# The last six chunks' product with w_out by one level of Strassen's algorithm

## The chip, the cores and the metric

The kernel runs on one core of a Trainium2 chip. The metric is the time on the device in microseconds (us). The engines work side by side, each through its own list in order: PE (TensorE, matrix products), DVE (VectorE), ACT (ScalarE), POOL (GpSimd) and SP (SyncE, which here only starts transfers).

## The reference

An attention over 4 batches, 8 heads, 768 positions and 64 values per head. Three of the heads see all earlier positions, the others only the first 4 and a window of 64. Its output, laid out as 3072 tokens by 512, goes through two dense products with a gate between them:

```python
def _moe_ref(x, w_in, w_out, beta):
    h = x @ w_in                                   # 3072x512 @ 512x2048
    g = h * (1.0 / (1.0 + np.exp(-beta * h)))
    return (g @ w_out).astype(np.float32)          # 3072x2048 @ 2048x512
```

The change concerns only the last line.

## The kernel before

The 3072 tokens are 8 chunks (NCHUNK) of 384, each a half of a batch's positions, so three tiles of 128 tokens. Each chunk has four units of attention (a unit is a pair of heads). For a unit `steps_QK` makes scores on PE and their exponentials on ACT, DVE multiplies masks into them (L509 to L527), `steps_PV` multiplies with the values, and `normalize` divides on DVE (`rec`, `x`, L572 and L576).

The first dense product, `steps_G1`, has 16 steps per chunk, one for each 128 of the 2048 columns (FO = 16 blocks): four matmuls of 384 columns into a bank of PSUM (L631), a tanh on ACT (`th`, L636), and the "gate" on DVE (L639), which writes the block `fi` of `gT[c]`, a bf16 tile of 128 x 16 x 384. A bank is free again after its gate. The second product, `steps_G2`, has four steps per token tile, each of four matmuls of 512 columns over four blocks (L684); after the fourth, ACT copies the bank to `osb` (L688) and SP stores it (L690). The very last tile is cut in 256, 128 and 128 columns (L669, L675, L677). Factor 0.5 in these copies belongs to the gate's formula.

PSUM has three pools: `ps_m` with three banks ("mm"), `ps_s` with two double banks ("sp"), `ps_o` with one.

The order of the work on every engine is written out by hand. `RAMP` is the list of words for the start, and `PLAN` has one line for each unit from unit 8 on: `V` a visit of scores, `p` a product with the values, `a` or `A` a step of the first product (with a bank of `ps_m` or `ps_s`), `b` a step of the second. `feed` takes the next step of the list `first` or `second`; where a `b` finds no step ready it runs an `a`, and the other way round. Gates, masks and loads are put off by `later` by a delay in the plan's own clock, which counts the steps' nominal costs, and a step that needs them runs them first. POOL makes the copies of values (`VX`, `VO`, L253 to L262) and issues the row loads of the next chunk's keys and queries (L284); SP issues the transposes, loads of v and stores.

## Time and profile before

| what | us |
|---|---|
| median of three runs | 228.47 (228.04 to 228.51) |
| profiled execution: span from the first to the last instruction | 226.6 |
| PE busy in it | 220.1 |
| ACT, DVE, POOL busy | 154.4, 138.7, 87.7 |
| matmuls of the second product with 512 columns (368) | 85.9 busy |
| granted PE clock over the span | 1.000 |

The profiled execution's own time is not given beside its span; the median is 1.9 us above it. A matmul's busy time is from its start to the end of its results, and the next one starts before that, so that 368 matmuls of 379 ns each took less than 368 x 379 ns of the time line. "Idle before" in a row of a group is the time that the engine waited ahead of these instructions, and behind the arrow stands whom it waited for. The chain is followed back from the last instruction through whatever ended last at each step.

### The profile page before, as it was taken

The page shows a single profiled execution, that of the slowest core. Times are in us where ns is not written, and L with a number is a line of the kernel's source. Part 1 is how long each engine was busy: PE and PEld are TensorE (multiplying, and loading weights), DVE is VectorE, ACT ScalarE, POOL GpSimd, SP SyncE. Part 2 cuts the span into 40 slices and gives each one's busy share as a digit, 9 for nine tenths or more (in the row PEclk, how much of TensorE's full clock was granted, in tenths as well). Part 3 has the DMA queues.
Part 4 walks back from the last instruction along what each step waited for, and adds up shares of the span by engine and source line. Part 5 has one row for each costly group of instructions (what it writes and reads, how often), then busy time and mean ns, then how long its engine had stood idle before and what let it go on. Part 6 is the DMA issues. An engine that isn't in the chain of part 4 may idle for free.

```text
span 226.6 us, 5028 instructions
## 1 busy us (share of the span) xinstructions
PE 220.1 (97%) x1918; PEld 126.5 (56%) x1918; DVE 138.7 (61%) x341; ACT 154.4 (68%) x253; POOL 87.7 (39%) x139
## 2 busy tenths in 40 slices
PE   8889999999999999999999999999999999999993
PEld 3556666644655665556644665556645565456553
DVE  2578898862674779357932699457854768038600
ACT  4689788846768897449933887669875887148521
POOL 4578940459272399143069019930520000000000
PEclk9999999999999999999999999999999999999999
DMA  6999999999999799999779986999704030110012
GB/s 205 253 307 226 201 209 232 197 223 178 145 211 179 159 158 140 126 188 155 86 132 153 152 192 77 127 157 144 178 4 127 4 81 0 49 74 19 0 56 87
DMA packets 95384, 31.67 MB, mean 140 GB/s; under 512 B 81776, under 2 KB 92416, under 8 KB 95360
## 3 DMA queue, kind: packets, MB, share of 16 engines
q1 hardware_dynamic: 58880, 22.82, 50.1%
q0 software_dynamic: 35904, 8.13, 41.3%
q10 hardware_dynamic: 576, 0.40, 0.5%
q8 instruction: 15, 0.25, 0.5%
q14 instruction: 9, 0.07, 0.1%
HBM read 27.27 MB, written 6.29 MB: 148 GB/s over the span
## 4 chain that ended last, share of the span: by engine, by line
PE 87%; DMA 6%; SPq 3%; POOL 1%; issue 0%; ACTq 0%; ACT 0%; POOLq 0%
PE mm L684 36%; PE mm L631 24%; PE sp L631 12%; PE po L563 6%; PE sp L482 6%; DMA vs<-in_v_dram 5%; DMA s<-in_q_dram 2%; PE mm L669 2%; SPq L133 1%; SPq L120 1%; PE mm L482 1%; PE mm L353 1%; PE mm L601 1%; POOL VX L253 1%; POOL VO L262 0%
## 5 line engine op out<-in xcount | busy, mean ns | idle before, releaser
L684 PE MATMUL mm<-w_out_sb,gT 128*128 128x512 bf16 x368 | 85.9, 379 | 0.0
L491 ACT ACTIVATE es<-sp 128x768 bf16<-128x768 f32 (+2 forms) x72 | 56.5, 834 | 18.3 <-PE sp L482 18.0
L631 PE MATMUL mm<-xT,w_in_sb 128*128 128x384 bf16 x348 | 64.5, 326 | 0.0
L631 PEld LDWEIGHTS <-w_in_sb 128*128 128x128 bf16 x512 | 47.8, 98 | 29.7 <-issue 0.2
L636 ACT ACTIVATE th<-mm,beta_h 128x384 f32<-128x384 f32 x87 | 49.6, 587 | 6.4 <-DVE Mh L238 1.0
L684 PEld LDWEIGHTS <-gT 128*128 128x128 bf16 x368 | 33.4, 98 | 36.0 <-issue 1.5
L639 DVE SCALAR_TENSOR_TENSOR gT<-th,mm 128x384 bf16<-128x384 f32 x87 | 46.8, 552 | 7.6 <-ACT th L636 3.8
L631 PE MATMUL sp<-xT,w_in_sb 128*128 128x384 bf16 x164 | 32.3, 326 | 0.0
L688 ACT ACTIVATE osb<-mm 128x512 f32<-128x512 f32 x23 | 13.8, 602 | 25.5 <-PE mm L684 25.2
L563 PEld LDWEIGHTS <-es 128*128 128x128 bf16 x472 | 23.5, 98 | 12.5 <-issue 0.9
L253 POOL CAST VX<-vs 128x512 bf16<-128x512 f32 x15 | 9.4, 627 | 51.6 <-DMA vs<-in_v_dram 42.0
L639 DVE SCALAR_TENSOR_TENSOR gT<-th,sp 128x384 bf16<-128x384 f32 x41 | 22.3, 552 | 5.7 <-ACT th L636 3.7
L636 ACT ACTIVATE th<-sp,beta_h 128x384 f32<-128x384 f32 x41 | 23.8, 586 | 2.3 <-PE sp L631 0.2
L563 PE MATMUL po<-VX,es 128*128 128x65 bf16 x360 | 25.1, 194 | 0.0
L284 POOL DMA_DIRECT2D s<-in_q_dram x30 | 22.5, 779 | 4.0 <-DMA w_out_sb<-in_moe_w_out_dram 4.0
L284 POOL DMA_DIRECT2D s<-in_k_dram x30 | 22.3, 757 | 3.6 <-DMA w_in_sb<-in_moe_w_in_dram 3.4
L572 DVE RECIPROCAL rec<-po 128x6 f32<-128x6 f32 x28 | 5.4, 192 | 28.0 <-PE po L563 27.9
L482 PE MATMUL sp<-QTD,KT 64*128 64x128 bf16 (+2 forms) x258 | 18.9, 240 | 0.0
L509 DVE TENSOR_TENSOR es<-es,Mh 128x768 bf16<-128x768 bf16 (+1 forms) x26 | 15.6, 628 | 5.0 <-ACT es L491 4.4
L576 DVE TENSOR_TENSOR x<-po,rec 128x384 bf16<-128x384 f32 x28 | 15.6, 557 | 1.0
L482 PEld LDWEIGHTS <-KT 64*128 64x128 bf16 x278 | 11.1, 94 | 5.7 <-issue 3.7
L261 POOL COPY VO<-VX 128x512 bf16<-128x512 bf16 x16 | 9.7, 629 | 6.0 <-DVE VX L253 6.0
(74 smaller groups left out, 156.1 us busy)
## 6 DMA issues: line engine op xcount, KB each, us to landing
vs<-in_v_dram SPq DMA_DIRECT2D x24, 256.0 KB, 5.3
out_dram<-osb SPq DMA_DIRECT2D x23, 256.0 KB, 2.8
w_in_sb<-in_moe_w_in_dram POOLq DMA_DIRECT2D x4, 512.0 KB, 9.6
w_out_sb<-in_moe_w_out_dram POOLq DMA_DIRECT2D x4, 512.0 KB, 17.0
s<-in_k_dram POOLq DMA_DIRECT2D x30, 64.0 KB, 4.3
s<-in_q_dram POOLq DMA_DIRECT2D x30, 64.0 KB, 5.7
s<-in_k_dram SPq DMA_DIRECT2D x4, 384.0 KB, 10.4
s<-in_q_dram SPq DMA_DIRECT2D x4, 384.0 KB, 10.5
```

The source lines that it names most:

```text
L253: copy(out=VX[b % 2][:, h2 * HT + t, :, 0:D], in_=staged["v", c][:, t])
L284: nc.gpsimd.dma_start(out=ROWS[c % 2, name][:, t, i * 4 * D:(i + 1) * 4 * D].rearrange("p (h d) -> p h d", d=D), in_=src[b, i:H:2, r:r + 1 ...
L482: nc.tensor.matmul(sps[i][r][:, x * 128:y * 128], key(a, lhs), s["QT"][half(a), qi * 128:(qi + y - x) * 128], start=first, stop=first or y ...
L491: nc.scalar.activation(out=views[i].rearrange("p r k j -> p r (k j)"), in_=banks[2][:, :, 0:n * 128], func=ACTF.Exp, scale=scale)
L509: eng.tensor_mul(ev[:, :, 0:n], ev[:, :, 0:n], Mh[h2][:, None, m0:m0 + n].to_broadcast([128, 2, n, 128]))
L563: nc.tensor.matmul(po[:, qi, hh, :], e, val, start=(j == 0), stop=(j == len(lst) - 1))
L576: nc.vector.tensor_mul(xg[g][:, :, :, u % 2, :].rearrange("p a t d -> p t a d"), po[:, :, :, 0:D], rec.to_broadcast([128, HT, 2, D]))
L631: nc.tensor.matmul(hp[:, 0:HALF], w_in_sb[:, mo, fi * 128:(fi + 1) * 128], xT[c][:, mo, :], start=(mo == 0), stop=(mo == MO - 1))
L636: nc.scalar.activation(out=th, in_=hp[:, 0:HALF], func=ACTF.Tanh, scale=beta_h[:, fi:fi + 1])
L639: nc.vector.scalar_tensor_tensor(out=gTs[c][:, fi, :], in0=th, scalar=1.0, in1=hp[:, 0:HALF], op0=ALU.add, op1=ALU.mult)
L684: nc.tensor.matmul(op, gTs[c][:, fi, ns * 128:(ns + 1) * 128], w_out_sb[:, fi, :], start=(fi == 0), stop=(fi == FO - 1))
L688: nc.scalar.activation(out=osb, in_=op, func=ACTF.Copy, scale=0.5)
```

## The change

The tokens of chunks 2 to 7 (18 tiles) are multiplied with w_out in nine pairs of tiles. With the pair's two tiles as the upper and lower half of a matrix A, cut in its 2048 columns at the middle (A11, A12 above, A21, A22 below), and w_out cut to B11, B12, B21, B22 of 1024 x 256 each, seven products of 256 columns take the place of eight:

- p1 = A11 B11, then p2 adds A12 B21 into the same bank X: ACT copies X after p1 (half of it is needed alone) and again after p2.
- p6 = S2 T2, then p7 adds N3 T3 into the same bank Y: DVE reads Y after p6 and after p7.
- p5 = S1 T1 into bank Z; p4 = A22 T4 into bank W; p3 adds N4 B22 into Z.

S1 = A21 - A22, S2 = A11 - S1, N3 = A21 - A11 and N4 = A12 - S2 are tensor_tensor operations of 128 x 1024 bf16 on DVE, made per pair by `minus`. The results are put together in `osb` by `plus`, five DVE operations of 128 x 256 per pair (in0 from PSUM, in1 from osb). T1 = B12 - B11, T2 = T1 + B22 (in two halves) and T4 = B21 - T2 are made once, by the new words ws0, ws1 and ws2 in unit 11's line of `PLAN`; T3 = B12 + B22 overwrites B12 at the first pair's start.

Tiles 0 and 1 of a chunk are a pair, and tile 2 of an even chunk goes with tile 2 of the next one. To keep it until then, POOL copies it to `kept` (128 x 2048 bf16) after the even chunk's pair has been issued. The last two pairs are taken step by step in turn. Per pair there are 7 steps of 8 matmuls, 63 steps for these tiles in place of 72 of 4. The loads, the first product and the attention are untouched; `osb` gets a fourth buffer, and two masks share buffers with the new sums.

The diff, with some lines around the edits left out:

```diff
     moe = ctx.enter_context(tc.tile_pool(name="moe", bufs=2))
+    sums = ctx.enter_context(tc.tile_pool(name="sums", bufs=3))
...
 
-    Ns = consts.tile([128, 5 * 128], BF16, name="Ns")
-    Nc = consts.tile([128, 256], BF16, name="Nc")
+    Ns = sums.tile([128, 8 * 128], BF16, name="S")[:, 0:5 * 128]
+    Nc = sums.tile([128, 8 * 128], BF16, name="S")[:, 0:256]
...
                                          start=(fi == 0), stop=(fi == FO - 1))
-                        osb = moe.tile([128, d_model], F32, name="osb", bufs=3)[:, 0:z - a]
+                        osb = moe.tile([128, d_model], F32, name="osb", bufs=4)[:, 0:z - a]
...
-                    osb = moe.tile([128, d_model], F32, name="osb", bufs=3)
+                    osb = moe.tile([128, d_model], F32, name="osb", bufs=4)
...
         return res
 
+    KB = FO // 2
+    wB11, wB12 = w_out_sb[:, 0:KB, 0:256], w_out_sb[:, 0:KB, 256:512]
+    wB21, wB22 = w_out_sb[:, KB:FO, 0:256], w_out_sb[:, KB:FO, 256:512]
+    wT = {}
+    def weight_sums(i):
+        sub = nc.vector.tensor_sub
+        if i == 0:
+            a = stage.tile([128, 2, 4, HT, D], F32, name="s0").rearrange("p n h t d -> p (n h t d)").bitcast(BF16)
+            b = stage.tile([128, 2, 4, HT, D], F32, name="s1").rearrange("p n h t d -> p (n h t d)").bitcast(BF16)
+            wT[1] = [a[:, 0:KB * 256].rearrange("p (f d) -> p f d", f=KB)]
+            wT[4] = [b[:, 0:KB * 256].rearrange("p (f d) -> p f d", f=KB)]
+            wT[2] = [x[:, KB * 256:KB * 384].rearrange("p (f d) -> p f d", f=KB // 2) for x in (a, b)]
+            sub(out=wT[1][0], in0=wB12, in1=wB11)
+        elif i in (1, 2):
+            f = slice((i - 1) * KB // 2, i * KB // 2)
+            nc.vector.tensor_add(out=wT[2][i - 1], in0=wT[1][0][:, f], in1=wB22[:, f])
+            sub(out=wT[4][0][:, f], in0=wB21[:, f], in1=wT[2][i - 1])
+        elif i == 3:
+            nc.vector.tensor_add(out=wB12, in0=wB12, in1=wB22)
+    def weight(n, kb):
+        return {"B11": lambda: w_out_sb[:, kb, 0:256], "T3": lambda: w_out_sb[:, kb, 256:512],
+                "B21": lambda: w_out_sb[:, KB + kb, 0:256], "B22": lambda: w_out_sb[:, KB + kb, 256:512],
+                "T1": lambda: wT[1][0][:, kb], "T4": lambda: wT[4][0][:, kb],
+                "T2": lambda: wT[2][kb // (KB // 2)][:, kb % (KB // 2)]}[n]()
+    kept = {}
+    def keep(c):
+        for f in gates[c]:
+            f()
+        kept[c] = moe.tile([128, FO, 128], BF16, name="kept", bufs=1)
+        nc.gpsimd.tensor_copy(out=kept[c], in_=gTs[c][:, :, 256:384])
+    def steps_seven(lo, hi, before=None, end=False, last=False):
+        h = {}
+        def place_of(x):
+            c, ns = x
+            return (2 * chunks[c][0] + chunks[c][1]) * HALF + ns * 128
+        def sides():
+            for c in (lo[0], hi[0]):
+                for f in gates[c]:
+                    f()
+            if lo[0] in kept:
+                A1 = kept.pop(lo[0])
+            else:
+                A1 = gTs[lo[0]][:, :, lo[1] * 128:(lo[1] + 1) * 128]
+            A2 = gTs[hi[0]][:, :, hi[1] * 128:(hi[1] + 1) * 128]
+            h.update(A11=A1[:, 0:KB], A12=A1[:, KB:FO], A21=A2[:, 0:KB], A22=A2[:, KB:FO])
+        def minus(n, a, b):
+            home = att.tile([128, 8 * 128], BF16, name="es", bufs=11) if end else sums.tile([128, 8 * 128], BF16, name="S")
+            h[n] = home.rearrange("p (f t) -> p f t", f=KB)
+            nc.vector.tensor_sub(out=h[n], in0=h[a], in1=h[b])
+        def mm(p, a, w, first=True, cols=(0, 256)):
+            if first and p not in h:
+                h[p] = ps_m.tile([128, 512], F32, name="mm")[:, 0:cols[1] - cols[0]]
+            for kb in range(KB):
+                nc.tensor.matmul(h[p], h[a][:, kb], weight(w, kb)[:, cols[0]:cols[1]], start=first and kb == 0, stop=kb == KB - 1, skip_group_check=not first)
+        def plus(out, p, other):
+            nc.vector.scalar_tensor_tensor(out=out, in0=h[p], scalar=0.5, in1=other, op0=ALU.mult, op1=ALU.add)
+        def store(x, osb, a=0, z=d_model):
+            n0 = place_of(x)
+            nc.sync.dma_start(out=out[n0:n0 + 128, a:z], in_=osb[:, a:z])
+        def p1():
+            if before is not None:
+                before()
+            sides()
+            h["o1"] = moe.tile([128, d_model], F32, name="osb", bufs=4)
+            h["o2"] = moe.tile([128, d_model], F32, name="osb", bufs=4)
+            mm("X", "A11", "B11")
+            nc.scalar.activation(out=h["o2"][:, 256:512], in_=h["X"], func=ACTF.Copy, scale=0.5)
+            minus("S1", "A21", "A22")
+            minus("S2", "A11", "S1")
+        def p2():
+            mm("X", "A12", "B21", first=False)
+            nc.scalar.activation(out=h["o1"][:, 0:256], in_=h["X"], func=ACTF.Copy, scale=0.5)
+            minus("N3", "A21", "A11")
+        def p6():
+            mm("Y", "S2", "T2")
+            plus(h["o1"][:, 256:512], "Y", h["o2"][:, 256:512])
+        def p7():
+            mm("Y", "N3", "T3", first=False)
+            plus(h["o2"][:, 0:256], "Y", h["o2"][:, 256:512])
+            minus("N4", "A12", "S2")
+        def p5():
+            mm("Z", "S1", "T1")
+            plus(h["o2"][:, 256:512], "Z", h["o2"][:, 0:256])
+        def p4():
+            mm("W", "A22", "T4")
+            plus(h["o2"][:, 0:256], "W", h["o2"][:, 0:256])
+            store(hi, h["o2"])
+        def p3():
+            mm("Z", "N4", "B22", first=False)
+            plus(h["o1"][:, 256:512], "Z", h["o1"][:, 256:512])
+            store(lo, h["o1"])
+        def p5_last():
+            zz = ps_s.tile([128, 2, 512], F32, name="sp")
+            for i in range(2):
+                h[f"Z{i}"] = zz[:, i, 0:128]
+                mm(f"Z{i}", "S1", "T1", cols=(i * 128, i * 128 + 128))
+                plus(h["o2"][:, 256 + i * 128:384 + i * 128], f"Z{i}", h["o2"][:, i * 128:i * 128 + 128])
+            store(hi, h["o2"], 256, 512)
+        def p4_last():
+            mm("W", "A22", "T4")
+            plus(h["o2"][:, 0:256], "W", h["o2"][:, 0:256])
+            store(hi, h["o2"], 0, 256)
+            store(lo, h["o1"], 0, 256)
+        def p3_last():
+            for i in range(2):
+                mm(f"Z{i}", "N4", "B22", first=False, cols=(i * 128, i * 128 + 128))
+                o = h["o1"][:, 256 + i * 128:384 + i * 128]
+                plus(o, f"Z{i}", o)
+                store(lo, h["o1"], 256 + i * 128, 384 + i * 128)
+        return [(8 * 109, f) for f in ((p1, p2, p6, p7, p5_last, p4_last, p3_last) if last else (p1, p2, p6, p7, p5, p4, p3))]
     first, second = [], []
     for c in range(NCHUNK):
         first += [(c, x) for x in steps_G1(c)]
-        second += [(c, x) for x in steps_G2(c)]
+        if c < 2:
+            second += [(c, x) for x in steps_G2(c)]
+        elif c % 2 == 0:
+            second += [(c, x) for x in steps_seven((c, 0), (c, 1), before=(lambda: weight_sums(3)) if c == 2 else None)]
+            second[-1] = (c, (second[-1][1][0], lambda f=second[-1][1][1], c=c: (f(), keep(c))))
+        elif c < NCHUNK - 1:
+            second += [(c, x) for x in steps_seven((c, 0), (c, 1))]
+            second += [(c, x) for x in steps_seven((c - 1, 2), (c, 2))]
+        else:
+            two = steps_seven((c - 1, 2), (c, 2), end=True), steps_seven((c, 0), (c, 1), end=True, last=True)
+            second += [(c, x) for both in zip(*two) for x in both]
 
...
             late[n].pop(0)(copies[eng or "v"])
+        elif what == "ws":
+            weight_sums(n)
...
-        A b A a V ro4 p V a p p ro4 p p p
+        A ws0 b A a V ro4 p V a ws1 p p ro4 ws2 p p p
         b A ro4 a a p V p ro4 p p ro4 b ro4 a a A ro4 A b b b dk4 A V a p dq4 p b A b
```

In the order of the built programs, line numbers of the new one stand a line or more behind the old ones (L631 is L632 there, L684 is L685, L639 is L640). At the second pair (chunk 3, tiles 0 and 1), PE ran this before: the last step of the first product, then steps of the second, with a product of the attention (po) in between.

```order
L631 LDWEIGHTS w_in_sb
L631 MATMUL sp<-xT,w_in_sb 128x384
L684 LDWEIGHTS gT
L684 MATMUL mm<-w_out_sb,gT 128x512 [waits DVE_49]
...
L563 LDWEIGHTS es
L563 MATMUL po<-VX_127,es 128x65
```

Now PE at the same place; the first L766 rows are p1, the one that waits for ACT (Activation_49) is p2's first, the rows with S are p6 (weights from S2, columns from T2 in s_1203), and the last two p7's first.

```order
L564 MATMUL po<-VX_130,es 128x65 [waits PE_49]
L766 LDWEIGHTS gT
L766 MATMUL mm<-w_out_sb,gT 128x256
...
L766 MATMUL mm<-w_out_sb,gT 128x256 [waits Activation_49]
...
L766 LDWEIGHTS S [waits DVE_49]
L766 MATMUL mm<-s_1203,S 128x256
...
L766 LDWEIGHTS S [waits DVE_49]
L766 MATMUL mm<-w_out_sb,S 128x256 [waits DVE_49]
```

Where one step of 512 columns followed another without a wait, p2 now waits for ACT, p6 for DVE's sum, and p7 for DVE's read, with nothing between these products.

DVE at the first pair (chunk 2, tiles 0 and 1) before: the end of a unit (rec and x), the last gate, the next unit's end, and masks.

```order
L572 RECIPROCAL rec<-po 128x6 [waits PE_49]
L576 TENSOR_TENSOR x<-po,rec 128x3x2x64 [waits DVE_49]
L639 SCALAR_TENSOR_TENSOR gT<-th,mm 128x384 [waits Activation_49]
L572 RECIPROCAL rec<-po 128x6 [waits PE_49]
L576 TENSOR_TENSOR x<-po,rec 128x3x2x64 [waits DMAHW7_49,DVE_49]
L509 TENSOR_TENSOR es<-es,Mh_112 128x768 [waits Activation_49] x2
```

And now: L721 is T3, L760 the block sums (S1, S2, N3, and N4 further down), L769 the reads of banks.

```order
L577 TENSOR_TENSOR x<-po,rec 128x3x2x64 [waits DVE_49]
L721 TENSOR_TENSOR w_out_sb<-w_out_sb 128x8x256
L640 SCALAR_TENSOR_TENSOR gT<-th,mm 128x384 [waits Activation_49]
L760 TENSOR_TENSOR S<-gT 128x1024 [waits DVE_49]
L760 TENSOR_TENSOR S<-gT,S 128x1024 [waits DVE_49]
L760 TENSOR_TENSOR S<-gT 128x1024
L769 SCALAR_TENSOR_TENSOR osb<-mm,osb 128x256 [waits DMAHW6_49,PE_49,Activation_49]
L573 RECIPROCAL rec<-po 128x6 [waits PE_49]
L577 TENSOR_TENSOR x<-po,rec 128x3x2x64 [waits DMAHW7_49,DVE_49]
L769 SCALAR_TENSOR_TENSOR osb<-mm,osb 128x256 [waits DMAHW5_49,PE_49]
L760 TENSOR_TENSOR S<-gT,S 128x1024
L510 TENSOR_TENSOR es<-es,Mh_115 128x768 [waits Activation_49] x2
```

T3 stands ahead of the last gate, and two reads of banks and four sums stand ahead of the masks (L510).

POOL at the same place before: the copies of values, then row loads.

```order
L261 COPY VO_129<-VX_127 128x8x64 [waits Pool_49]
L262 COPY VO_129<-VX_127 4x8x64 [waits Pool_49]
L284 DMA s_558<-in_k_dram 128x4x64 [waits DMAHW7_49,DMASW2_49]
L284 DMA s_558<-in_k_dram 128x4x64 [waits DMAHW0_49,DMASW3_49]
L284 DMA s_558<-in_k_dram 128x4x64 [waits DMASW4_49]
L284 DMA s_558<-in_k_dram 128x4x64 [waits DMASW5_49]
```

And now, with `kept`, which waits for the chunk's last gate:

```order
L262 COPY VO_132<-VX_130 128x8x64 [waits Pool_49]
L263 COPY VO_132<-VX_130 4x8x64 [waits Pool_49]
L285 DMA s_561<-in_k_dram 128x4x64 [waits DMAHW7_49,DMASW2_49]
L285 DMA s_561<-in_k_dram 128x4x64 [waits DMAHW0_49,DMASW3_49]
L736 COPY kept<-gT 128x2048 [waits DVE_49]
L285 DMA s_561<-in_k_dram 128x4x64 [waits DMASW4_49]
```

The row loads behind it start when the copy has ended.

## The prediction

> **What bounds the kernel now.** I read the busy times first, then the chain that ended last, then one window over the stretch that the change touches.
>
> ```profile
> PE 220.1 (97%) x1918; PEld 126.5 (56%) x1918; DVE 138.7 (61%) x341; ACT 154.4 (68%) x253; POOL 87.7 (39%) x139
> ...
> PE 87%; DMA 6%; SPq 3%; POOL 1%; issue 0%; ACTq 0%; ACT 0%; POOLq 0%
> ...
> L684 PE MATMUL mm<-w_out_sb,gT 128*128 128x512 bf16 x368 | 85.9, 379 | 0.0
> ```
> ```profile
> 88.50:222.90 134.40, 134.34 (x1110) 76.03 (x1107) 77.53 (x188) 85.97 (x142) 35.87 (x50) 1.00 0.71 101
> ```
>
> TensorE (PE) carries 87% of the chain. From 88.5 us, where chunk 2 starts its product with w_out, to 222.9 us it is busy 134.34 of 134.40 us at the full granted clock (1.00). So every microsecond of matmul taken away there is gained, and every microsecond that PE has to wait is lost: nothing absorbs it. VectorE (DVE) has 77.5 us of work in these 134 us.
>
> **The matmuls saved.** The chain in order of time and the instructions of the last tile price the columns:
>
> ```profile
> 212.41 6.91 PE mm L684 x32
> 219.31 3.55 PE mm L669 x48
> ```
> ```profile
> L669 PE MATMUL mm<-w_out_sb,gT x48: 219/219/273, 219.1 to 222.6; 128*128 128x128 bf16 x32, 128*128 128x256 bf16 x16
> ```
>
> 32 matmuls of 512 columns take 6.91 us, 0.216 each. The last tile's 16 of 256 and 32 of 128 columns take 3.55; with 0.109 and 0.056 they make 1.75 + 1.79 = 3.54, so price goes by columns and a narrow matmul pays no extra for its weights. A pair of token tiles costs 32 x 0.216 = 6.91 now, and 7 products x 8 x 0.109 = 6.12 then: 0.79 saved, nine times 7.1, and 0.1 more because the last tile's split costs less: **-7.2 us**. A rule speaks against this term: the Trainium skill, "TensorE: Matmul & The Clock Gate", section "Back-to-back issue gap", gives about 81 ns for a pair of weight load and matmul at 128 columns and 131 ns at 512. An estimate halfway by columns is 98 ns at 256, and by these a pair would get dearer, 5.5 us in place of 4.2. The rows above (0.216 and 0.056) disagree with it at both ends, so the sum does not use it; as a rival it stands below.
>
> **What the seven products wait for.** I call the pairs 1 to 9 in the order of the program: 1 = chunk 2 tiles 0,1; 2 = chunk 3 tiles 0,1; 3 = tile 2 of both; 4 to 6 the same for chunks 4 and 5; 7 = chunk 6 tiles 0,1; 8 and 9 interleaved at the end. PE takes its instructions in order, so a product that waits holds up all behind it.
>
> *First term: p2 adds into p1's bank.* ScalarE (ACT) must first copy the half-finished bank. In pairs 1 to 6 p2 stands directly behind p1.
>
> ```profile
> 219.15 3.70 PE L669 MATMUL mm<-w_out_sb,gT 128*128 128x256 bf16 x48
> 221.10 0.39 ACT L677 ACTIVATE osb<-mm 128x256 f32<-128x256 f32 x1 [1.15 <-PE mm L669]
> ```
> ```profile
> 7.54 0.48 ACT L364 COPY QTD<-mm 128x384 bf16<-128x384 bf16 x1 [0.39 <-PE mm L353]
> 8.14 0.28 PEld L482 LDWEIGHTS <-KT 64*128 64x128 bf16 x10 [0.42 <-ACT QTD L364]
> ```
>
> The sixteenth 256-column matmul could be followed by another at 219.15 + 1.75 = 220.90; it ends 0.16 later (273 ns long against 109 ns of spacing), and the copy starts at 221.10 and takes 0.39. From the end of an ACT copy (7.54 + 0.48) to the PE instruction that waited are 0.12. Gap: 0.16 + 0.04 + 0.39 + 0.12 = 0.71. In pair 4 two exponentials stand ahead of the copy on ACT:
>
> ```profile
> L491 ACT ACTIVATE es<-sp 128x768 bf16<-128x768 f32 x48 | 37.2, 810 | 14.4 <-PE sp L482 14.1
> ```
>
> With the first still running when p1 begins and a shorter one behind it I take 1.2 there. Pair 7 has two short matmuls in between: 0.65. Pairs 8 and 9 cover each other. 5 x 0.7 + 1.2 + 0.65 = **+5.35**.
>
> *Second term: p7 adds into p6's bank*, which DVE must have read (a scalar_tensor_tensor of 256 columns).
>
> ```profile
> L639 DVE SCALAR_TENSOR_TENSOR gT<-th,mm 128x384 bf16<-128x384 f32 x87 | 46.8, 552 | 7.6 <-ACT th L636 3.8
> L675 DVE TENSOR_SCALAR osb<-mm 128x128 f32<-128x128 f32 x1 | 0.3, 291 | 8.4 <-PE mm L669 8.4
> ```
> ```profile
> 12.97 0.39 DVE L248 CAST qkb<-s 128x384 bf16<-128x384 f32 x1 [1.02 <-DMA s<-in_k_dram]
> 13.41 0.17 PEld L353 LDWEIGHTS <-qkb 128*128 128x128 bf16 x3 [0.88 <-DVE qkb L248]
> ```
>
> 384 columns take 0.552 and 128 take 0.291, so 256 take 0.42. DVE to PE is 13.41 - 13.36 = 0.05, PE to DVE about the same. Gap: 0.16 + 0.06 + 0.42 + 0.05 = 0.7. p7 is directly behind p6 in pairs 2, 3, 5, 6, 7 (3.5); pair 4 has four tiny matmuls between (0.6); pair 1 has attention work of over 1 us there (0); in 8 and 9 the block sums of the other pair keep DVE back (0.5): **+4.6**. The third such place, p3 behind p5, has p4 (0.87 us) between: DVE needs 0.2 + 0.42 + 0.69 + 0.42 = 1.73 after p7, and p3 comes at 1.75; nothing, with no reserve.
>
> *Third term: the block sums come late for p6.* S1 needs the chunk's last gate, S2 needs S1. The three gate rows at the present start of such a stage:
>
> ```profile
> 212.24 5.34 PE L684 MATMUL mm<-w_out_sb,gT 128*128 128x512 bf16 x24
> 212.44 0.58 ACT L636 ACTIVATE th<-sp,beta_h 128x384 f32<-128x384 f32 x1
> 213.06 0.55 DVE L639 SCALAR_TENSOR_TENSOR gT<-th,sp 128x384 bf16<-128x384 f32 x1
> ```
> ```profile
> L509 DVE TENSOR_TENSOR es<-es,Mh x26: 420/554/1676, 21.2 to 186.7; 128x768 bf16<-128x768 bf16 x21, 128x512 bf16<-128x512 bf16 x5
> ```
>
> The last gate ends 1.37 us after the product begins. That is hidden now, since the product wants the gates one by one. A bf16 sum of 768 columns is 0.55 us undisturbed and of 512 is 0.42, so 1024 is 0.69. S1 and S2 end 1.37 + 2 x 0.72 = 2.85 after p1 began; p1, gap and p2 end at 0.87 + 0.71 + 0.87 = 2.45. Pair 2 waits 0.45. In pairs 5 and 7 an x of the attention delays the gates: 0.9 and 0.45. Pairs 3 and 6 need no new gate: 0. Pair 1 has DVE's sum T3 over w_out (2048 columns, 1.22 us by the same slope) and these two ahead of the last gate:
>
> ```profile
> 89.01 0.19 DVE L572 RECIPROCAL rec<-po 128x6 f32<-128x6 f32 x1
> 89.24 0.56 DVE L576 TENSOR_TENSOR x<-po,rec 128x384 bf16<-128x384 f32 x1
> ```
>
> rec and x end 0.9 after p1 begins, T3 at 2.1, the gate at 2.65, S2 at 4.05: 1.6. Together **+3.4**. Behind p5 of pair 1 stand products that need a mask which on DVE comes after two of the new operations (0.42 + 0.69): **+0.95**.
>
> *Fourth term: the copy "kept" on GpSimd (POOL)*, 2048 columns, in pairs 1, 4 and 7. It waits for the same last gate as S1.
>
> ```profile
> 139.16 2.41 DVE L509 TENSOR_TENSOR es<-es,Mh 128x768 bf16<-128x768 bf16 x2
> 139.62 1.68 POOL L262 COPY VO<-VX 4x1536 bf16<-4x1536 bf16 x1
> ```
> ```profile
> 108.09 0.91 DVE L509 TENSOR_TENSOR es<-es,Mh 128x768 bf16<-128x768 bf16 x2
> ```
> ```profile
> L262 POOL COPY VO<-VX 4x1536 bf16<-4x1536 bf16 x4 | 6.1, 1516 | 0.2
> L261 POOL COPY VO<-VX 128x512 bf16<-128x512 bf16 x16 | 9.7, 629 | 6.0 <-DVE VX L253 6.0
> ```
>
> Two mask products take 0.91 us alone and 2.41 beside a POOL copy of 1.68: the second of them ended only after the copy did, 1.50 lost. By 629 ns for 512 columns and 1516 for 1536 the new copy is 1.96. The Trainium skill, "SBUF — State Buffer", section "Who interferes with whom", calls the port pair an exclusive lock between a DVE operation with two SBUF inputs and a GpSimd operation that reads SBUF; by it S2 would lose the whole 1.96 in pairs 1 and 7, 3.9 in place of the 3.0 I take by the row's delay. Worked from the rows alone, the bounds are 0 and 2 x 1.96 = 3.9, and I take the measured delay of 1.50 for pair 1 and pair 7 each (pair 4 none: DMA issues keep POOL from starting the copy beside the sums). **+3.0**.
>
> *The rest.* T1, T2, T4 (five operations on DVE, 1.22 + 4 x 0.69 = 4.0 us) go into the stretch of
>
> ```profile
> 60.00:70.00 10.00, 10.00 (x126) 6.04 (x125) 7.68 (x21) 6.97 (x12) 5.74 (x7) 1.00 1.22 177
> ```
>
> where it has 2.3 us free: 0 to 1.7 over, I take **+0.5**. Two ACT reads of 256 replace two of 512 per pair, off the path: 0. POOL's row loads start up to 2 us later behind "kept"; before they are used lie a whole chunk's steps: 0, at most 1. The plan of steps keeps its words while the products have 63 steps for these tiles in place of 72, so a few b words run a step of the first product instead: the same PE work earlier, 0. Stores carry the same bytes from four buffers instead of three: 0. The last one waits for a DVE read of 128 columns (0.29) as now for ACT's:
>
> ```profile
> 222.93 0.28 ACT L677 ACTIVATE osb<-mm 128x128 f32<-128x128 f32 x1 [1.45 <-PE mm L669]
> ```
>
> **Sum.** -7.2 + 5.35 + 4.6 + 3.4 + 0.95 + 3.0 + 0.5 = +10.6. It is made on the profiled execution's span of 226.6, which lies 1.9 below the median of 228.47 (what is around the span), so the median becomes 239.1; I say 239.
>
> **Rivals.**
> 1. *Only the bank handovers cost* (terms one and two), because sums and copies find DVE idle: -7.2 + 9.95 = +2.75, 231.2 (229 to 233.5). For it: DVE has 57 us free after 88.5 us. Against: the gate rows, since S1 cannot begin before 1.37. Chance 0.22.
> 2. *Faster:* the handover at p2 and p7 is short. If PE's drain and the signals vanish behind each other, the thirteen gaps cost their 0.4 us of read alone, 5.2, and sums are on time: -2.0, 226.5. It decides at 0.8 us of waiting per pair. Against: in the handover rows the read stands whole, with 0.04 to 0.12 on either side of it. Chance 0.10, of which a tenth ends nearer than 0.2%.
> 3. *DVE becomes the bound of the attention too.* It gets 36 sums x 0.69, 45 reads x 0.42 and T3: 45 us on top of 77.5, 122 of some 140. If each of the 16 units after pair 1 then waits for its masks another 0.3 to 0.5, 5 to 8 more: 245. For it: the mask in pair 1. Against: PE's own waits give DVE time. Chance 0.08.
> 4. *Narrow matmuls bound by their weights:* at the LDWEIGHTS share of 126.5 us for 1918, 66 ns on average, a 256 would need over 0.12 to undo the saving; then 0.8 a pair is gone, 246. L669 speaks against it. Chance 0.02. (The rule on the issue gap above would be this one.)
>
> My forecast, 233.5 to 243.5, has 0.58. Measurement tells 0.2% (0.45 us) from no change. Faster: 0.10 less the near part, and a little of rival 1: 0.10; same 0.03; slower 0.87. The range 229.5 to 244 leaves out rival 2 and the upper rivals, 0.19; the likeliest case's own is 233.5 to 243.5.
>
> **What would show it.** Right: PE idle ahead of the 256-column products, released by ACT about 0.7 us at p2 and by DVE at p6 and p7; the matmuls themselves 9 x 0.79 shorter; DVE sums of over 1.5 us beside POOL's three copies of about 2 us; the window from 88.5 to the end some 10 us longer and DVE near 85% there. Wrong: PE gaps of 0.3 us or less at p2, or sums of 0.7 us beside the copies (then rival 1 or 2); the granted clock below 1.00 after a long wait, which no row here prices.

## The result and the profile after

The changed kernel takes 257.53 us (257.23 to 258.62, four runs), the kernel before 228.49 on the same chip: 1.128 times as long (95% interval 1.126 to 1.131). The forecast was 239, between 229.5 and 244. The direction was right; of +29 us it had +10.6.

The page of the changed kernel: busy times, the granted PE clock in 40 slices, and the chain that ended last.

```profile
PE 223.4 (87%) x2113; PEld 148.2 (58%) x2118; DVE 187.0 (73%) x429; ACT 150.4 (59%) x252; POOL 95.2 (37%) x142
...
PEclk9999999999999997979999999979999999999998
...
PE 64%; DVE 16%; DMA 10%; issue 3%; ACT 3%; SPq 1%; ACTq 0%; POOL 0%; DVEq 0%
```

The window from the first of the seven products to 0.4 us behind the last matmul (which ends at 252.5), the counterpart of 88.50 to 222.90 before. Behind its length stand the busy times of PE, PEld (weight loads), DVE, ACT and POOL, each with the number of instructions, then the granted PE clock, the DMA share and GB/s:

```profile
91.20:252.90 161.70, 137.44 (x1310) 97.79 (x1308) 122.69 (x271) 82.36 (x142) 45.53 (x56) 0.97 0.58 84
```

It is 27.3 us longer (161.70 against 134.40; 26.9 without the 0.4 at the end), and PE, which was idle 0.06 us there, now waits 23.9. DVE has 122.7 us of work, the 122 that the third rival gave it. The clock, 1.00 before, is 0.97 over this stretch, with dips in single slices. Whom PE waited for over the whole span (line, releaser: total us, times, longest):

```profile
PE mm L766 <- DVE S L760: 4.9, 4, 2.7
PE mm L766 <- DVE osb L769: 4.1, 7, 0.8
PE mm L766 <- ACT osb L782: 3.4, 7, 0.7
PE mm L632 <- DMA xT<-x: 2.7, 1, 2.7
PE sp L632 <- DMA xT<-x: 1.7, 1, 1.7
PE mm L632 <- DVE gT L640: 1.5, 1, 1.5
PE po L564 <- DVE x L577: 1.4, 1, 1.4
PE po L564 <- DVE es L510: 1.4, 2, 0.7
...
PE mm L766 <- DVE gT L640: 1.0, 2, 0.5
PE mm L602 <- DVE x L577: 1.0, 1, 1.0
PE sp L766 <- DVE osb L769: 0.8, 2, 0.4
PE po L564 <- DVE es L524: 0.7, 1, 0.7
...
PE mm L632 <- DVE xT L611: 0.3, 1, 0.3
```

The row of a matmul ends 0.16 us after the next one could have started, as in the prediction, so each wait cost 0.16 more than it shows. Sorted by the prediction's terms:

| term | forecast | measured |
|---|---|---|
| matmuls saved | -7.2 | -7.2 (the spacing of 0.109 stands, below) |
| p2 behind ACT's copy | 5.35 | 3.4 + 7 x 0.16 = 4.5 |
| p7 (and products of the last two pairs) behind DVE's read of a bank | 4.6 | 4.1 + 0.8 + 9 x 0.16 = 6.3 |
| p6 behind the block sums, the copy `kept` included | 3.4 + 3.0 | 4.9 + 4 x 0.16 = 5.5 |
| a late last gate ahead of p1 or p2 | in the row above | 1.0 + 2 x 0.16 = 1.3 |
| products with the values behind masks | 0.95 | 1.4 + 0.7 + 3 x 0.16 = 2.6 |
| the weight sums ws0 to ws2 (at 73.8 us) | 0.5 | 1.4 + 0.16 = 1.6 |
| first product behind xT | 0 | 2.7 + 1.7 + 2 x 0.16 = 4.7 |
| first product behind gates, the last x and its transposes | 0 | 1.5 + 1.0 + 0.3 + 3 x 0.16 = 3.3 |
| half clock | not priced | at most 3 x 3.41 / 2 = 5.1 |

The sum is 27.7; the span grew by 29.5 (256.1 against 226.6), so 1.8 are short waits and the like that I did not assign. The rows that were in the forecast come to 21.8 of waits where it had 17.8. The other 13.1 are the first product's waits and the clock, and these had a zero or no price.

Pair 1, all engines in order of time: POOL's copy beside DVE's second sum, and p6 behind it. A row gives start and length in us, engine, line, operation, tiles, shapes and count, and in brackets how long the engine was idle before it and whom it waited for. The view ends at 98 us and has four of p6's eight matmuls.

```profile
94.17 0.69 DVE L760 TENSOR_TENSOR S<-gT 128x1024 bf16<-128x1024 bf16 x1
...
94.20 2.41 POOL L736 COPY kept<-gT 128x2048 bf16<-128x2048 bf16 x1 [1.98 <-DVE gT L640]
...
94.89 2.26 DVE L760 TENSOR_TENSOR S<-gT,S 128x1024 bf16<-128x1024 bf16 x1
...
97.21 1.04 PE L766 MATMUL mm<-s,S 128*128 128x256 bf16 x4 [2.73 <-DVE S L760]
```

S2 takes 2.26 in place of 0.69 and ends 0.54 after the copy: 1.57 lost, where the forecast had 1.50.

A wait that the forecast did not have, 10 us later in the same way of reading. SP has the stores of the pair (L773) and a load of v ahead of the transpose of x (SPq are SP's issues):

```profile
105.08 2.05 SPq L773 DMA_DIRECT2D out_dram<-osb  x2
...
105.65 0.56 DVE L577 TENSOR_TENSOR x<-po,rec 128x384 bf16<-128x384 f32 x1
...
107.18 0.43 SPq L134 DMA_DIRECT2D vs<-in_v_dram  x1
...
107.66 1.39 SPq L592 DMA_TRANSPOSE xT<-x  x1
...
108.07 0.50 PE L632 MATMUL mm<-xT,w_in_sb 128*128 128x384 bf16 x2
...
111.24 0.80 PE L632 MATMUL mm<-xT,w_in_sb 128*128 128x384 bf16 x2 [2.67 <-DMA xT<-x]
```

x is ready at 106.2, its transpose starts 1.45 later, and PE comes to chunk 3's first product 0.4 after that. The second half of xT lands 2.8 us too late (3.17 less two matmuls of 0.16). From 111.24 on, matmuls of 384 columns are 0.32 us apart instead of 0.162: half clock. The granted clock around such places:

```profile
93.75:97.16 3.41, 0.28 (x1) 0.10 (x1) 3.34 (x4) 0.38 (x1) 2.96 (x2) 1.00 0.59 99
107.40:110.82 3.42, 1.17 (x19) 0.71 (x19) 1.67 (x4) 1.30 (x2) 0.26 (x1) 1.00 0.95 224
165.43:168.84 3.41, 1.43 (x16) 0.78 (x13) 3.27 (x8) 1.34 (x3) 3.41 (x5) 1.00 1.20 228
```
```profile
97.10:100.60 3.50, 3.39 (x35) 2.62 (x35) 1.08 (x3) 0.20 (x1) 3.17 (x5) 0.51 0.92 62
```

In the three windows PE was busy 0.28, 1.17 and 1.43 of 3.41 us. Behind each the clock is 0.50 for 3.41 us: the fourth row is the one behind the first.

### The profile page after: what moved, and what is told of

It is laid out like the page before. It is cut to its first block, busy times and chain, and to the rows that moved or that the text cites. A ratio compares the mean times of both kernels' runs of the same rounds, so it can differ in the third digit from the quotient of the medians.

```text
span 256.1 us, 5549 instructions
## 1 busy us (share of the span) xinstructions
PE 223.4 (87%) x2113; PEld 148.2 (58%) x2118; DVE 187.0 (73%) x429; ACT 150.4 (59%) x252; POOL 95.2 (37%) x142
## 4 chain that ended last, share of the span: by engine, by line
PE 64%; DVE 16%; DMA 10%; issue 3%; ACT 3%; SPq 1%; ACTq 0%; POOL 0%; DVEq 0%
PE mm L632 19%; PE mm L766 17%; PE sp L632 10%; PE mm L685 6%; PE sp L483 5%; PE po L564 5%; DVE gT L640 4%; DVE S L760 3%; DMA w_in_sb<-in_moe_w_in_dram 3%; DMA xT<-x 3%; DVE osb L769 3%; DMA s<-in_k_dram 2%; DMA s<-in_q_dram 2%; DVE x L577 1%; SPq L134 1%
## 5 line engine op out<-in xcount | busy, mean ns | idle before, releaser
L632 PE MATMUL mm<-xT,w_in_sb 128*128 128x384 bf16 x356 | 67.5, 330 | 4.5 <-DMA xT<-x 2.7
L632 PEld LDWEIGHTS <-w_in_sb 128*128 128x128 bf16 x512 | 48.4, 99 | 39.0 <-issue 10.5
L640 DVE SCALAR_TENSOR_TENSOR gT<-th,mm 128x384 bf16<-128x384 f32 x89 | 47.6, 551 | 11.4 <-ACT th L637 8.0
L632 PE MATMUL sp<-xT,w_in_sb 128*128 128x384 bf16 x156 | 31.8, 335 | 2.6 <-DMA xT<-x 1.7
L769 DVE SCALAR_TENSOR_TENSOR osb<-mm,osb 128x256 f32<-128x256 f32 x43 | 18.1, 422 | 16.3 <-PE mm L766 12.2
L766 PEld LDWEIGHTS <-S 128*128 128x128 bf16 x224 | 21.1, 99 | 13.7 <-DVE S L760 6.0
L637 ACT ACTIVATE th<-sp,beta_h 128x384 f32<-128x384 f32 x39 | 22.5, 586 | 6.1 <-PE sp L632 3.4
L640 DVE SCALAR_TENSOR_TENSOR gT<-th,sp 128x384 bf16<-128x384 f32 x39 | 21.1, 551 | 4.6 <-ACT th L637 2.8
L685 PE MATMUL mm<-w_out_sb,gT 128*128 128x512 bf16 x91 | 22.1, 379 | 0.4 <-issue 0.2
L736 POOL COPY kept<-gT 128x2048 bf16<-128x2048 bf16 x3 | 6.7, 2231 | 35.6 <-DVE gT L640 35.6
L766 PEld LDWEIGHTS <-gT 128*128 128x128 bf16 x168 | 15.9, 98 | 6.8 <-issue 4.0
L766 PE MATMUL mm<-s,S 128*128 128x256 bf16 x112 | 15.4, 283 | 4.9 <-DVE S L760 4.9
L766 PE MATMUL mm<-w_out_sb,S 128*128 128x256 bf16 x112 | 14.5, 272 | 3.7 <-DVE osb L769 3.7
```

The source lines that it names most:

```text
L632: nc.tensor.matmul(hp[:, 0:HALF], w_in_sb[:, mo, fi * 128:(fi + 1) * 128], xT[c][:, mo, :], start=(mo == 0), stop=(mo == MO - 1))
L637: nc.scalar.activation(out=th, in_=hp[:, 0:HALF], func=ACTF.Tanh, scale=beta_h[:, fi:fi + 1])
L640: nc.vector.scalar_tensor_tensor(out=gTs[c][:, fi, :], in0=th, scalar=1.0, in1=hp[:, 0:HALF], op0=ALU.add, op1=ALU.mult)
L685: nc.tensor.matmul(op, gTs[c][:, fi, ns * 128:(ns + 1) * 128], w_out_sb[:, fi, :], start=(fi == 0), stop=(fi == FO - 1))
L766: nc.tensor.matmul(h[p], h[a][:, kb], weight(w, kb)[:, cols[0]:cols[1]], start=first and kb == 0, stop=kb == KB - 1, skip_group_check=not ...
L769: nc.vector.scalar_tensor_tensor(out=out, in0=h[p], scalar=0.5, in1=other, op0=ALU.mult, op1=ALU.add)
```

## The experiments

All times are medians in us, beside the kernel before on the same chip (228.4 to 228.8). Line numbers of the variants differ by a few. The edits are printed in short form, with comments and names such as `nothing` or `go` in place of longer code.

### The handovers: another order of the products (e4)

```diff
+        def q4():
+            mm("W", "A22", "T4")
+            plus(h["o2"][:, 0:256], "W", h["o2"][:, 256:512])
+        def q5():
+            mm("Z", "S1", "T1")
+            minus("N4", "A12", "S2")
+            plus(h["o2"][:, 256:512], "Z", h["o2"][:, 256:512])
+        def q7():
+            mm("Y", "N3", "T3", first=False)
+            plus(h["o2"][:, 0:256], "Y", h["o2"][:, 0:256])
+            plus(h["o2"][:, 256:512], "Y", h["o2"][:, 256:512])
+            store(hi, h["o2"])
-        (p1, p2, p6, p7, p5, p4, p3)
+        (p1, q4, p2, p6, q5, q7, p3)
```

> In pairs 1 to 7 the products come in the order p1, p4, p2, p6, p5, p7, p3, so that another product stands between the two that share a bank; DVE gets one more operation of 256 columns per pair (0.42). My first two terms: the seven waits for ACT (4.6 together) and six for DVE (4.7) go, and S2 has 0.87 more time in four pairs (2.9); 257.5 becomes 245.5 (243 to 249). Theory B (DVE is the bound): the waits come back at the sums and the masks, with 2.9 more of DVE work: 255 to 259.

Measured 247.44 (ratio 1.083, 1.079 to 1.086): 10 less than the changed kernel, inside the range that counts the first two terms and S2's share (243 to 249). No row of a wait for ACT's copy is left. The longest are now:

```profile
PE mm L632 <- DMA xT<-x: 2.9, 1, 2.9
PE sp L632 <- DMA xT<-x: 2.5, 1, 2.5
PE mm L766 <- DVE S L760: 1.7, 2, 1.0
PE mm L766 <- DVE osb L769: 1.7, 4, 0.8
```

With 0.16 for each, ACT's 4.5 went, 2.9 of the waits for DVE's reads and 3.5 of those for the sums, 10.9 together. So the handovers were real, and with one more product ahead of them the sums came in time in more pairs; one more DVE read per pair did not eat the gain. Theory B in its plain form (PE waits for DVE wherever the work stands) fails here.

### The copy `kept`, later (e3), and the stores, later (e2)

```diff
-        nc.gpsimd.tensor_copy(out=kept[c], in_=gTs[c][:, :, 256:384])
+        keeping[c] = later(3000, go)      # go: the tensor_copy
```

> POOL's copy kept is issued 3 us of the plan's clock later, when S1 and S2 are done. If the copy holds up DVE's sums and half clock follows a wait of about 3 us: S2 takes 0.69 in place of 2.26 us in pairs 1 and 7, p6 waits 1.4 in place of 2.91 and 0 in place of 1.52, the half clock from 97.2 us (1.7) goes; 257.5 becomes 252.8 (251 to 255). If only the copy's lock counts and not the clock: 254.5. If S2 was long for another reason: 257.5 within 1.

Measured 257.67, no gain. The lock itself is as expected: with the copy gone from its side S2 is short,

```profile
93.79 0.69 DVE L762 TENSOR_TENSOR S<-gT,S 128x1024 bf16<-128x1024 bf16 x1
```

p6 of pair 1 waits 1.2 in place of 2.7, and no half clock follows there. But PE then runs into the waits for xT sooner: the second grows from 1.7 to 3.4, and around the first stand 6.8 us of half clock instead of 3.4. What was gained at one place was handed to the next. Pair 7 stayed as it was (S2 2.26, p6 waits 1.35): POOL had been idle for 36 us there, so the copy still started with the last gate, and an issue that stands later in the program moved nothing.

```diff
-            nc.sync.dma_start(out=out[...], in_=osb[:, a:z])
+            later(4000, lambda: nc.sync.dma_start(out=out[...], in_=osb[:, a:z]))
```

> The stores of pairs 1 to 7 are put 4 us of the plan's clock later in SP's queue, behind the transposes. If stores that wait for DVE hold back the transposes behind them: the wait of 2.83 us at 111 us goes with its half clock (1.7), and of the 1.87 at 168 us about 0.5; 257.5 becomes 252.5 (251 to 254). If x itself is late on DVE: no change, 257.5 within 1.

Measured 255.29 (ratio 1.117, 1.111 to 1.122): 2.2 less. The wait at 111 us falls from 2.7 to 0.5 and the one at 168 us goes, both with their half clock, so SP's stores did hold the transposes back; but p6's waits grow (7.4 together in place of 4.9), and one half clock appears behind them at 182.7.

### The steps: an empty eighth (e1), own third tile (e5, e6)

```diff
-        return [p1, p2, p6, p7, p5, p4, p3]
+        return [p1, p2, p6, p7, p5, p4, p3, nothing]
```

> An eighth step that does nothing is put behind each of pairs 1 to 7, so that a word b of the plan meets the same number of steps as before. Theory A (the seven steps in place of eight pull steps of the first product ahead, in front of their transposed x): the two waits of the first product for xT, 2.83 and 1.87 us in the changed kernel, go, with the stretches of half clock that follow them (1.7 each) and the 1.66 that a first product then waits for gates at 176 us; 257.5 becomes 249 (246 to 253). Theory B (DVE has too much to do, everything waits for it wherever it stands): 257 within 1, the waits move and stay.

Measured 258.42, no gain, and the waits for xT grow:

```profile
PE mm L632 <- DMA xT<-x: 7.9, 2, 4.7
```

My reading of the missing steps was wrong in this form. A step without matmuls takes none of PE's time, so PE only comes sooner to the first product, whose x is no earlier. My reading since is that the transposes need PE's time between x and the first product, not a count of words; e12 below tests it.

```diff
         elif c < NCHUNK - 1:
             second += steps_seven((c, 0), (c, 1))
-            second += steps_seven((c - 1, 2), (c, 2))     # odd chunks
+            second += steps_G2(c)[8:12]                   # tile 2 of its own chunk, chunks 2 to 5
```

> Tile 2 of chunks 2 to 5 goes by the old four steps behind its own chunk's pair; pairs 3 and 6 and the copies kept of chunks 2 and 4 fall away, T3 has its own buffer (three operations, 1.5 in place of 1.2 us). Theory A (an even chunk had 12 steps to put between its attention's x and the next chunk's first product, and has 7 in the changed kernel, since its third tile was moved behind the next chunk's pair; so xT is wanted 4 us sooner): the waits for xT (4.7) go with their half clock (3.4), S2 of pair 1 is short again (1.6 and 1.7 of half clock), pairs 3 and 6 wait no more (2.75) but save nothing (1.6 lost), of the first product's waits at 166 to 176 us half goes (1.2): 257.5 becomes 243.7 (241 to 247). Theory B (x comes late because DVE is behind with its work): the waits for xT stay; 253 (251 to 256).

Measured 254.64 (ratio 1.111, 1.104 to 1.118), far above the 247 that I allowed. The two waits went (0.3 and 0.2 are left of them), but a new one came at chunk 4's first product. Chunk 3 has 11 steps ahead of it now, 14 in the changed kernel and 12 in the kernel before:

```profile
131.74 0.49 PE L632 MATMUL sp<-xT,w_in_sb 128*128 128x384 bf16 x2
...
135.59 0.80 PE L632 MATMUL sp<-xT,w_in_sb 128*128 128x384 bf16 x2 [3.36 <-DMA xT<-x]
```

With 6.8 and 3.4 us of half clock, and 3.2 for a gate at 151 us, most of the gain was gone.

> e5 and e4's order of products together. If the two causes add up: e5's time less the waits at p2 (3.3), p7 (3.2) and for S2 (2.9) of the five pairs before the last two, 9.4: 234.5 (231 to 238). Theory B: not under 243.

e4 and e5 together: 244.82 (ratio 1.072, 1.071 to 1.074). Over 238: the wait at chunk 4 is there again (3.6). The two measured gains do add up, though: the 10 of e4 and the 3 of e5 off 257.5 would give 244.5, within e5's interval of the 244.82. The forecast was missed because it rested on e5's expected 243.7; with e5's measured 254.64 the same 9.4 gives 245.2.

### One part alone: the third tile moved (e12), the sums (e13)

e12 has the old matmuls; only the steps of tile 2 of the even chunks, with POOL's copy for them, stand where the changed kernel has them. Its buffers are the changed kernel's, as in e11 below, which takes 228.5 with them.

```diff
         elif c % 2 == 0:
+            second += steps_G2(c)[0:8]      # and POOL's copy kept
         else:
+            second += steps_G2(c)[0:8] + steps_G2(c - 1)[8:12] + steps_G2(c)[8:12]
```

> The kernel before, all products by the old matmuls of 512 columns, with only the third tile of chunks 2, 4 and 6 moved behind the first two tiles of the next chunk, and POOL's copy kept for it; no sums on DVE. Theory A (fewer steps between the attention's x and the next first product): PE reaches chunk 3's first product 3.45 us sooner, at 98.4 in place of 101.8, its xT lands at about 101: 2.6 of waiting, perhaps with 1.7 of half clock; chunk 5's xT had 3.6 more slack: 0 to 0.5. 231.5 (230 to 234). Theory B (only DVE's late x makes PE wait for xT): 228.2 to 229.2.

Measured 239.57 (ratio 1.049, 1.046 to 1.053): 11.0 more than before, without a sum on DVE and without one of the seven products. Around chunk 3's first product, all engines in order of time:

```profile
96.09 0.56 DVE L577 TENSOR_TENSOR x<-po,rec 128x384 bf16<-128x384 f32 x1
...
96.67 1.22 SPq L592 DMA_TRANSPOSE xT<-x  x1
...
97.39 0.49 PE L632 MATMUL mm<-xT,w_in_sb 128*128 128x384 bf16 x2
...
100.27 1.08 PE L632 MATMUL mm<-xT,w_in_sb 128*128 128x384 bf16 x3 [2.40 <-DMA xT<-x]
```

and the same in the kernel before:

```profile
96.20 0.56 DVE L576 TENSOR_TENSOR x<-po,rec 128x384 bf16<-128x384 f32 x1
...
96.79 1.21 SPq L591 DMA_TRANSPOSE xT<-x  x1
...
101.81 0.81 PE L631 MATMUL sp<-xT,w_in_sb 128*128 128x384 bf16 x4
```

x and its transpose come at the same time, the first product 4.4 us sooner: four steps of 0.86, and attention work that now stands behind it. The data lands 3.6 us after the transpose started. Chunk 5 waits in the same way (2.25 with the 0.16), where I had allowed 0.5, and each wait is followed by half clock. With 1.3 for a gate at 161 us, 1.5 at the last x and 3.4 of clock this is about the 11.0. It is more than Theory A's 230 to 234, by chunk 5, the gate and the clock, and by the same mechanism; Theory B's 229.2 is excluded.

e13 has the sums and nothing else:

```diff
+                    for n in {0: ("S1", "S2"), 4: ("N3",), 12: ("N4",)}.get(f0, ()):
+                        t = sums.tile([128, 8 * 128], BF16, name="S")
+                        nc.vector.tensor_sub(out=t, in0=..., in1=...)
```

> The kernel before, all products by the old matmuls, with the 36 block sums and the weight sums also made on DVE and read by nothing: DVE's extra load without moved steps, bank handovers or copies by POOL. Theory A: waits at masks, gates and behind the weight sums, 3 to 5 together, none over 1 for xT: 232.5 (231 to 234). Theory B: x comes late enough that PE waits 3 or more for xT, with half clock: 235 to 238. If DVE's idle time takes the sums in: 228.4 to 229.5.

Measured 235.09 (ratio 1.027, 1.023 to 1.030): 6.5 more, just inside Theory B's range. The profiled execution took 233.20, inside Theory A's range, and it has none of Theory B's waits for xT; PE waited for masks and, at 72.4 us, behind the weight sums:

```profile
PE po L564 <- DVE es L510: 3.3, 2, 2.2
PE po L564 <- DVE x L577: 1.4, 1, 1.4
```

With 3 x 0.16 this is 5.2, and the profiled span is 4.9 longer than before. The other three took 235.05 to 235.55 at a granted clock of 0.991 to 0.992 against 0.998 here: they had about 1.5 us of half-clock loss more, and no trace shows behind which wait. So for them a late xT isn't excluded. The larger mask wait (2.17) is one where a sum of 0.69 took 1.95 beside a copy of values of 1.80 on POOL.

### What xT's waits cost altogether, and fewer sums (e8, e9)

> e4 with one thing taken away: the first product of chunks 3 to 6 reads 384 columns of w_in where it read xT, so it never waits for a transpose (its result is not the reference's; all instructions, transposes too, stay). Theory A: e4's two waits for xT (3.09 and 2.66) and the two stretches of half clock behind them (1.7 each) go, 9.1 together: 247.4 becomes 238.3 (236 to 241). Rival: PE would only run into the next late thing (the gates, the masks), which DVE does no sooner: 244 to 247.

```diff
-                nc.tensor.matmul(hp, w_in_sb[...], xT[c][:, mo, :], ...)
+                nc.tensor.matmul(hp, w_in_sb[...], w_in_sb[:, mo, 0:HALF], ...)   # chunks 3 to 6
```

Measured 240.99 (ratio 1.055, 1.052 to 1.058): 6.5 less than e4, inside the range. No half clock is left before the end. Of the 9.1 expected 2.6 came back, among it a wait of 1.2 for a gate at 159 us and 0.6 for S2 in pair 5: the rival in small.

> e4 without two of the four block sums of each pair: N3 and N4 are left out and S1 and S2 read in their place (so p7 and p3 are not the reference's products). DVE has 12.4 us less to do. Theory A (the order, not DVE's load, sets the waits for xT): only the waits for masks (0.67, 0.88, 0.64, 0.60) and at p3 (0.43, 0.95) shrink, 247.4 becomes 243.7 (242 to 246). Theory B (DVE's load makes x late): the waits for xT shrink too by 3 and their half clock goes: 237 to 241.

```diff
-            minus("N3", "A21", "A11")
+            h["N3"] = h["S1"]          # N4 = S2 likewise
```

Measured 244.88 (ratio 1.071, 1.067 to 1.075): 2.6 less than e4, with 12.4 us less of DVE work. The waits for xT stay:

```profile
PE mm L632 <- DMA xT<-x: 2.7, 1, 2.7
PE sp L632 <- DMA xT<-x: 2.4, 1, 2.4
```

So these 12.4 us of DVE's work did not make them, and e12 has such waits with no sum on DVE at all.

### The clock by itself (p1, p2)

The kernel before with one pause of PE ahead of chunk 7's second tile:

```diff
+                    for i in range(2):      # p1: range(1)
+                        nc.scalar.copy(out=w, in_=gTs[c][:, 0:8, 0:128])
+                    nc.tensor.matmul(po[:, 0:128], w[:, 0:128], w_out_sb[:, 0, 0:128])
```

> The kernel before, with one pause of PE put between the first and second tile of chunk 7's product with w_out: ACT makes two copies of 128 x 1024 that the next matmul waits for, together with the copy to osb about 3.0 us of pause. If the clock drops to half for 3.4 us after a pause of about 3 us: +3.0 and +1.7, 233.2. If the half clock in the changed kernel had another cause: +3.0, 231.5.

> As the pause of three, with one copy by ACT in place of two: a pause of about 1.9 us. If half clock follows only where nearly a whole stretch of 3.4 us was idle: +1.9 alone, 230.3. If any pause of this length brings it: +3.6, 232.

p2 measured 232.95 (ratio 1.020, 1.016 to 1.023), p1 230.30 (1.008, 1.005 to 1.011). The pauses in the profiles are 2.70 and 1.62, each with 0.16 more: 2.9 and 1.8. The longer cost 4.6, which is 2.9 + 1.7; the shorter 1.9 and nothing besides. Three of p2's four executions ran at a granted clock of 0.989 and took 232.68 to 233.60; the fourth ran at 1.000 and took 231.62, so the same pause came there without half clock. The windows of 3.41 us in p2:

```profile
215.70:219.11 3.41, 0.76 (x5) 0.41 (x6) 0.00 (x0) 2.56 (x3) 0.00 (x0) 1.00 0.20 77
219.11:222.52 3.41, 3.41 (x10) 1.18 (x9) 0.00 (x0) 0.00 (x0) 0.00 (x0) 0.50 0.02 5
```

and in p1:

```profile
214.91:218.32 3.41, 1.79 (x10) 0.66 (x8) 0.00 (x0) 1.53 (x2) 0.00 (x0) 1.00 0.20 77
218.32:221.70 3.38, 3.38 (x19) 1.76 (x18) 0.00 (x0) 0.34 (x1) 0.00 (x0) 1.00 0.02 5
```

### Where it pays (e7, e10, e11, e14)

> Seven products for tiles 0 and 1 of chunks 3 and 5 alone, in e4's order, all else as in the kernel before; the weight sums (5.5 us) in four stretches between 90 and 103 us where DVE was idle for 7.8. Theory A: 1.6 saved, 0.3 to 1.0 lost at the pairs and the sums: 227.5 (226.8 to 228.6), a little faster than before. Theory B (any work added to DVE between 90 and 190 us comes back as waits): 229.5 or more.

```diff
+        elif c in (3, 5):
+            second += steps_seven((c, 0), (c, 1)) + steps_G2(c)[8:12]    # e4's order
+        else:
+            second += steps_G2(c)
```

Measured 231.08 (ratio 1.012, 1.010 to 1.014), so 1.2% slower. In the profile the weight sums at their new place cost nothing, and the pairs wait 0.3 once for S2; but chunk 4's first product waits 1.6 for xT, as chunk 3 has 11 steps for 12, and another first product 0.8 for a bank. Even a saving without waits of its own brings the wait for xT.

At the end nothing waits for x any more:

> Seven products for tiles 0 and 1 of chunk 7 alone, at the very end, in e4's order and behind chunk 7's tile 2 by the old way, so that 3.45 us of matmuls cover the last gates and the first sums; the weight sums stand at 192 to 198 us, where DVE was idle. All else as before. My terms: 9.6 us of matmuls in place of 10.5 for the last three tiles, no wait: 227.6 (227.2 to 228.4). Rival (waits of 0.4 to 0.6 at p2, p7 or p3 also here, as in the changed kernel's last pairs): 228.5 to 229.5.

```diff
+            second += steps_G2(7)[8:12]                                   # tile 2 first
+            second += steps_seven((7, 0), (7, 1), end=True, last=True)    # e4's order; p5 and p3 in halves
```

Measured 229.58 (ratio 1.0044, 1.0030 to 1.0057). The two halves shared one PSUM tile, and the second waited for DVE's read of the first:

```profile
PE sp L769 <- DVE osb L772: 1.5, 2, 0.9
```

> e10 with the two halves of p5 and p3 in PSUM tiles of their own: in e10 they shared one tile, and the second half waited for DVE's read of the first, 1.03 and 0.76 us. If these two waits are all that undid the saving: 229.6 less 1.8, 227.8 (227.4 to 228.3), faster than before by 0.3%. If each only makes room for the next (p3 behind DVE's two reads of bank Y): 228.6 to 229.3.

Measured 228.52 against 228.61 (ratio 1.0005, 0.9983 to 1.0028), twelve runs: the waits are gone, and 32 matmuls of 256 columns take 3.49 us, 0.109 each, but no time is gained. SP has four stores at the end (start and length of the whole stretch of issues):

```profile
219.63 4.32 SPq L776 DMA_DIRECT2D out_dram<-osb  x4
```

```diff
-                store(lo, h["o1"], 256 + i * 128, 384 + i * 128)    # after each half
+            store(lo, h["o1"], 256, 512)                            # after both
```

> e11 with the last right half stored by one transfer in place of two. In e11 the matmuls after chunk 7's first product took 0.9 us less than before, but the last transfer was issued 0.5 later after the last matmul (SP had three stores in a row there). If that took back half of the saving: 0.4 less than e11, 0.3% under the kernel before, 227.9 (227.6 to 228.4). Rival (the end is set by the transfer's own time, larger for 128 KB than for 64): no change from e11, 228.5.

Measured 227.65 against 228.73 (ratio 0.9962, 0.9938 to 0.9986), twelve runs: 0.4% faster than the kernel before, with three stores:

```profile
219.91 3.82 SPq L776 DMA_DIRECT2D out_dram<-osb  x3
```

The issues take 0.5 us less. This one pair now brings 1.1 us, about the 0.9 that its matmuls save. That the step from e11 is the store's is likely but not sharp: 0.9 measured where the issues give 0.5, and each interval is some 0.5 us to either side.

## Why the prediction was right in direction and wrong in size

- *What bounds the kernel* was right: PE had no slack, and each wait came out as time. The direction was no luck: the waits of the forecast rows alone, 21.8, are three times the 7.2 saved.
- *The matmuls saved* (-7.2): right. The spacing of 0.109 holds for 256 columns wherever nothing waits, and the fourth rival fell.
- *First and second term*: p2 0.64 in most pairs where the sum had 0.71, p7 0.73 where it had 0.7. The second was low by 1.7, most of it since the last two pairs do not cover each other: three waits of about 0.55 there, where 8 and 9 had 0.5 together.
- *Third and fourth term*: 6.4 forecast, 5.5 measured, or 6.8 with the late gates. S2 lost 1.57 to the copy in pair 1 and the same in pair 7. Two readings behind the third term were off, and they partly cancel: by the rows shown rec and x end 1.3 after the product begins (88.50 to 89.80; 1.30 in the changed kernel too), not 0.9, which adds 0.4 to pair 1; and 1.37 + 2 x 0.72 is 2.81, not 2.85, so pairs 2 and 7 wait a little less.
- *Masks and weight sums*: 0.95 and 0.5 forecast, 2.6 and 1.6 measured. The mask of a later product in pair 1 and one in pair 4 wait just as the first did, and the weight sums fell right ahead of a rec and x for which PE waited. That "it has 2.3 us free" in a window of 10 says nothing of whether they are free where they are wanted.
- *The step that failed* stands under "The rest": "so a few b words run a step of the first product instead: the same PE work earlier, 0". It counted 63 steps for 72 and did not look where they are missing. Chunks 2 and 4 have 7 steps where they had 12, and chunk 3 and 5 get 14. These steps were the time in which the transposes of x landed: 4.4 us in e12, against the 3.6 that a transpose takes. The move alone, with its copy on POOL, cost 11.0 us (e12), more than a third of the loss. Beside it, "Stores carry the same bytes ... 0" was wrong too: they wait on SP for DVE, and the transpose waits behind them (e2: 2.2). In the changed kernel's wait at 111 us both act: 1.45 of its 2.83 us is the transpose's late start.
- *The granted clock* stood in the last part as that "which no row here prices". It was up to 5.1 of the 29 us, and p2 gives the price: 1.7 for a pause that fills most of a window of 3.41 us.
- *The rivals*: the first two fell with the 5.5 us behind the sums and with handovers of 0.64 and 0.73 us. DVE as the bound of the attention (245) came nearer than the forecast and had 0.08, but by a mechanism that e9 and e13 limit to 2.6 to 6.5 us. A rival on what the moved third tile uncovers was missing.

What stays open: the parts alone do not add up. The move (11.0), the sums (6.5) and the handovers (10, e4) less the 7.2 saved are 20 of 29 us. Where the remaining 9 arise was not measured. No run has DVE's reads of the banks (45 x 0.42) alone, or the sums beside the copy `kept`; and the parts can act on each other, since in e3 and e5 PE that waits less at one place came sooner to the next late x or gate.

## What to carry to other kernels

Work of the critical engine is also the cover under which transfers land: before it is cut or moved, list what arrives during it, with the slack of each, place by place and not as a count over the kernel. A trade of an eighth fewer matmul columns for more dependencies paid here only where other work, or another product, stood between each pair of dependent steps and nothing behind them waited for a transfer, as in the last stage here (0.4% won with one pair there, where nine pairs lost 12.8%). Count with the clock, too: a pause of TensorE that leaves it under 43% busy in one window of 3.41 us, about 2 us, cost 1.7 us of half clock behind it.
